# Moving the spectral pairs of batches 3 to 7 to fixed slots of a group

## The chip, the cores and the metric

The kernel runs on one core of one Trainium2 chip. The metric is the device time of one execution in microseconds (us); lower is better. Engines are named as in the profile: PE is TensorE (PEld its weight loads), DVE is VectorE, ACT is ScalarE, POOL is GpSimd and SP is SyncE. SP, ACT and POOL also issue the DMAs, each in the order of its own queue.

## The reference

Two blocks follow each other on x of 8 batches, 3136 positions and 256 channels. The first filters x along the sequence in the frequency domain; the second adds a low-rank product along the sequence and a two-layer network over the channels.

```python
def _attn_ref(x, filt_r, filt_i):
    X = np.fft.rfft(x, axis=1)
    F = (filt_r + 1j * filt_i)[None, :, :]
    return np.fft.irfft(X * F, n=x.shape[1], axis=1).astype(np.float32)

def _moe_ref(x, U, V, w_ch1, w_ch2):        # x is the first block's result
    xt = x.transpose(0, 2, 1)
    h = xt @ U @ V                          # U: 3136 x 32, V: 32 x 3136
    u = x + h.transpose(0, 2, 1)
    ch = np.maximum(u @ w_ch1, 0.0) @ w_ch2 # 256 -> 1024 -> 256
    return (u + ch).astype(np.float32)
```

## The kernel before

The Fourier transform of length 3136 = 64 x 49 is done as matrix products in float16, in stages. All of it is one instruction stream for each engine, whose order the kernel writes out by hand; nothing reorders it later.

**The stages of a batch.** `load_x` brings x in three chunks (POOL issues the DMAs). `f1_units` makes the first transform: one matmul into `pf` (L449) and one ACT copy (L455) per unit, 13 units, and after each chunk a store to the buffer `c1` in HBM (L459, from POOL). `load_a` (L468, from SP) reads `c1` back in another order, four blocks for each batch, all of which need the whole of `c1`. The middle stage takes 16 **pairs** of frequencies, four for each block. `stream` makes them one after another, and each pair consists of these steps:
- `forward`: two matmuls into `px` (L487), in a PSUM bank with the tag "x", of which there is one;
- `product`: three DVE multiplications with the filter read `px` (L506 once, L508 twice), and POOL adds the two halves to `y` (L511). Batch 1 uses `both_products` instead (one DVE instruction, L495);
- `i1`, two pairs later (`LAG = 2`): two matmuls with `y` into `pi` (L523), in the bank with the tag "f", of which there is one too, and an ACT copy to `esb` (L527). After four pairs SP stores `esb` to `c2` (L529).

`load_e` (L475, L480, from SP) reads `c2` back into the tiles `e2`. `h1_unit` then makes the batch's **low-rank sum** in three steps: 49 matmuls into `ph` (L563, also in the bank "f") and an ACT copy; a matmul and an ACT copy into `hz`; a DVE copy (L574) and four DMAs from SP (L580, L582, L585), which put the sum into rows 64 to 95 of `e2`.

**The groups.** The two-layer network goes over groups of 512 positions (8 rows of 64), six for each batch, and after each odd batch an **odd group** of the last row of two batches (128 columns). `make_u` builds u of a group (16 matmuls, L606, and two ACT copies). `mm1` makes one of eight blocks of hidden values: two matmuls into `phh` (L680) and a relu, on ACT (L688) or DVE (L686). The banks with the tag "m", of which there are four, hold `phh`, `pu`, `pf` and the second step's result. `mm2` makes the output of the group before in four steps. From batch 2 on it is `mm2_turned`, four matmuls in each step (L735); after its second and its fourth step DVE adds u (`tt`, L739) and transposes (L740), and after the fourth SP and POOL store the result. For batches 0 and 1 and for odd groups, `mm2` uses L706 and L710 and a DVE copy (L715); for an odd group only its first step does anything. The store of an odd group is two DMAs, one for each of its batches (L723).

**The order.** The main loop at the end of the kernel runs four steps for each group: `mm1` twice, `run(slot)`, in the third step `make_u` of the next group, a step of `mm2` of the group before, `run(slot + 1)`. So a full group has 8 slots, of which the even ones stand behind the two `mm1` and the odd ones behind the `mm2` step, and a batch has `SB = 48`. An odd group has no slots. What runs in a slot is put there in advance with `put`, and a slot runs its entries in the order in which they were put. The list `steps` holds the slot of each pair, from batch 1 on; the times of `load_a`, of `f1_units`, of `load_x` and of `load_e` are worked out from it, so that they move with it:

```python
for gi in range(NS // KG):
    t = steps[NP * (b - 1) + GP * gi]
    put(max(0, t - (14 if b > 3 else 9 + b // 3)), one(load_a, b, gi))
```

Before, the pairs of batch b stand in slots 48 (b - 2) + 18 + 3k, so that they take every slot of a group in turn. The low-rank sum's three steps stand 9, 8 and 7 slots ahead of the batch's first group.

Of the kernel before, what the change touches and what calls it, by code (L numbers as in the profile page):

```python
# [13 lines left out]
SEQ = 3136  # L14
NQ, NR = 64, 49
NS = 32
DM = 256
# [6 lines left out]
TB = 2  # L24
# [66 lines left out]
def kernel(  # L91
# [11 lines left out]
    nc = tc.nc  # L103
    nb = x.shape[0]
# [9 lines left out]
    RD = NR * DM  # L114
# [9 lines left out]
    def bank(tag, name):  # L124
        return ps.tile([128, 512], F32, tag=tag, bufs=BUFS[tag], name=name)
# [9 lines left out]
    def rows(ap, b, r, n):  # L135

        return bass.AP(tensor=ap.tensor, offset=ap.offset + (b * SEQ + r) * DM,
                       ap=[[RD, NQ], [1, n * DM]])

    def natural(ap):  # L140

        return ap.rearrange("p (r i h a) -> p r h i a", i=4, h=2, a=32)

    def split(ap):

        return ap.rearrange("p (r h i a) -> p r h i a", i=4, h=2, a=32)
# [104 lines left out]
    for h in range(2):  # L251
# [3 lines left out]
                    ap=[[64 * 1024, 4], [1024, 32], [1, 1024]]))  # L255
# [184 lines left out]
    def f1_units(b, both):  # L440
        ne = 0
        for c in range(len(CH)):
            xt = st[b]["x"].pop(c)
            asb = sb.tile([128, 9 * DM], F16, tag="asb", bufs=2, name="asb")
            for n0 in range(0, CH[c], 2):
                w = min(2, CH[c] - n0) * DM
                k = 64 if c0[c] + n0 == NH - 1 else 128
                pf = bank("o" if b == 1 else "m", "pf")
                nc.tensor.matmul(pf[:, 0:w], w64[:, :], xt[:, n0 * DM:n0 * DM + w],  # L449
                                 start=True, stop=True)  # L450
                dst = asb[0:k, n0 * DM:n0 * DM + w]
                if both and ne % 2 and (b > 1 or ne >= 9):
                    nc.vector.tensor_copy(dst, pf[0:k, 0:w])
                else:
                    nc.scalar.copy(dst, pf[0:k, 0:w])  # L455
                ne += 1
                if n0 + 2 >= CH[c]:
                    for h, o, n in span(c0[c], c0[c + 1]):
                        (nc.sync if b == 1 else nc.gpsimd).dma_start(c1[b].ap()[:, o:o + n], asb[64 * h:64 * h + 64, 0:n])  # L459
                yield  # L460
# [84 lines left out]
    def one(load, *a):  # L545
        load(*a)
        yield
# [78 lines left out]
    def turned(gx):  # L626

        return groups[gx][0] >= TB and groups[gx][2] > 1 and gx + 2 < len(groups)
# [46 lines left out]
    def mm1(gx, t):  # L675
        w = groups[gx][2] * 128
        ut = uts[gx]
        pm = bank("m", "phh")
        for dh in range(2):
            nc.tensor.matmul(pm[:, 0:w], w1[:, dh * 1024 + t * 128:dh * 1024 + (t + 1) * 128],  # L680
                             ut[:, dh * w:(dh + 1) * w], start=(dh == 0), stop=(dh == 1))
        h = sb.tile([128, 512], F16, tag="h", bufs=18, name="h")
        hs[gx, t] = h
        b = groups[gx][0]
        if t in ((4,) if b < TB or b == nb - 2 else () if b < nb - 1 else (1, 4, 6)):
            nc.vector.tensor_relu(h[:, 0:w], pm[:, 0:w])  # L686
        else:
            nc.scalar.activation(h[:, 0:w], pm[:, 0:w], RELU)  # L688

    def mm2(gx, rr):  # L690
        if gx < 0 or rr >= groups[gx][2]:
            return
        b, r0, nr = groups[gx]
        w = nr * 128
        if turned(gx):
            mm2_turned(gx, rr)
            return
        if rr == 0:
            ochs[gx] = (sb.tile([128, 4 * DM], F32, tag="och", bufs=2, name="och") if nr > 1 else
                        sb.tile([128, DM], F32, tag="ocho", bufs=1, name="ocho"))  # L700
        if rr % 2 == 0:
            pos[gx] = bank("o", "po")
        po, ut, och = pos[gx], uts[gx], ochs[gx]
        o = (rr % 2) * DM
        for t in range(8):
            nc.tensor.matmul(po[:, o:o + DM], hs[gx, t][:, rr * 128:(rr + 1) * 128],  # L706
                             w2[:, t * DM:(t + 1) * DM], start=(t == 0), stop=False,
                             skip_group_check=True)
        for dh in range(2):
            nc.tensor.matmul(po[:, o + dh * 128:o + (dh + 1) * 128],  # L710
                             ut[:, dh * w + rr * 128:dh * w + (rr + 1) * 128], idn[:, :],
                             start=False, stop=(dh == 1), skip_group_check=True)
        if rr % 2 or rr == nr - 1:
            a = (rr - rr % 2) * DM
            nc.vector.tensor_copy(natural(och[:, a:(rr + 1) * DM]), split(po[:, 0:(rr + 1) * DM - a]))  # L715
        if rr == nr - 1:
            for h in range(2):
                if nr == 1:
                    dst = rows(out, b - 1 + h, NR - 1, 1)
                else:  # L720
                    dst = rows(out, b, 2 * r0 + 4 * h, 4)
                eng = nc.gpsimd if b < nb - 1 else nc.scalar if gx + 2 >= len(groups) and h else nc.sync
                eng.dma_start(dst, och[64 * h:64 * h + 64, 0:nr * DM])  # L723

    def mm2_turned(gx, a):

        b, r0, _ = groups[gx]
        dh = a // 2
        if a == 0:
            ochs[gx] = sb.tile([128, 4 * DM], F32, tag="och", bufs=2, name="och")  # L730
        if a % 2 == 0:
            pos[gx] = bank("o", "po")
        po, och = pos[gx], ochs[gx]
        for t in range(4 * (a % 2), 4 * (a % 2) + 4):
            nc.tensor.matmul(po[:, :], w2[:, t * DM + dh * 128:t * DM + (dh + 1) * 128],  # L735
                             hs[gx, t][:, :], start=(t == 0), stop=(t == 7))
        if a % 2:
            tt = sb.tile([128, 512], F32, tag="tt", bufs=1, name="tt")
            nc.vector.tensor_add(tt, po[:, :], uts[gx][:, dh * 512:(dh + 1) * 512])  # L739
            nc.vector.transpose(och.rearrange("p (j h a) -> p h j a", h=2, a=32)[:, dh],  # L740
                                tt.rearrange("p (j t) -> p j t", t=32))
        if a == 3:
            for n in range(8):
                i, k = n // 2, n % 2
                dst = bass.AP(tensor=out.tensor,
                              offset=out.offset + (b * SEQ + 2 * r0) * DM + k * 32 * RD + i * 64,
                              ap=[[RD, 32], [DM, 8], [1, 64]])
                (nc.gpsimd if k and b < nb - 1 else nc.sync).dma_start(  # L748
                    dst, och[32 * i:32 * i + 32, k * 512:(k + 1) * 512]
                    .rearrange("p (r e) -> p r e", r=8))  # L750
# [3 lines left out]
    def put(slot, gen):  # L754
        sched.setdefault(int(slot + 0.5), []).append(gen)
# [6 lines left out]
    NP = NS // 2  # L762
    GP = NP // (NS // KG)
    SB = 48
# [17 lines left out]
    next(h1gen)  # L782
    make_u(0)

    steps = [7.6 + 1.3 * k for k in range(NP)] + [28 + 2.45 * k for k in range(NP)]
    for b in range(3, nb):
        steps += [SB * (b - 2) + 18 + 3 * k for k in range(NP)]
    steps += [steps[-1] + 3 * (k + 1) for k in range(LAG)]
    mid = stream()
    for k, t in enumerate(steps):  # L790
        put(t, mid)
        b, m = divmod(k - LAG, NP)
# [8 lines left out]
    for b in range(1, nb):  # L801
        for gi in range(NS // KG):
            t = steps[NP * (b - 1) + GP * gi]
            put(max(0, t - (14 if b > 3 else 9 + b // 3)), one(load_a, b, gi))
        gen = h1_unit(b)
        for t in (9, 8, 7):
            put(SB * b - t, gen)
        if b > 1:
            fill = f1_units(b, b == 2)
            t0 = steps[NP * (b - 1)]  # L810
            for k in range(NF):
                put(4 + 1.1 * k if b == 2 else 18 + 2.8 * k if b == 3 else t0 - 54 + 3 * k, fill)
            for c in range(len(CH)):
                if b > 2 or c > 0:
                    put(6 * c - 5 if b == 2 else 9 + 8 * c if b == 3 else t0 - 72 + 12 * c, one(load_x, b, c))
# [54 lines left out]
```

## Time and profile before

| | us |
|---|---|
| median of 3 runs | 544.36 |
| lowest and highest | 544.21, 546.55 |
| the profiled execution | 542.44 |
| its span, from the first to the last instruction | 540.7 |
| mean granted TensorE clock in it | 0.986 |

The profile shows one execution. Its busy times in stretches that end about where the low-rank sum of a batch stands (121 us for batch 1, 186 for batch 2, and so on, 475 for batch 7):

| stretch, us | length | PE busy | DVE busy | ACT busy | POOL busy | granted clock |
|---|---|---|---|---|---|---|
| 0 to 64 | 64 | 42.77 | 41.63 | 36.65 | 45.08 | 0.89 |
| 64 to 121 | 57 | 55.51 | 39.93 | 40.73 | 18.48 | 1.00 |
| 121 to 186 | 65 | 62.37 | 51.87 | 46.43 | 37.16 | 1.00 |
| 186 to 247 | 61 | 59.37 | 47.09 | 47.11 | 36.97 | 1.00 |
| 247 to 305 | 58 | 56.61 | 50.19 | 46.84 | 39.88 | 1.00 |
| 305 to 365 | 60 | 58.44 | 50.28 | 47.98 | 40.88 | 1.00 |
| 365 to 421 | 56 | 54.73 | 49.62 | 42.42 | 33.47 | 1.00 |
| 421 to 475 | 54 | 52.49 | 38.08 | 36.87 | 25.31 | 1.00 |
| 475 to 541 | 66 | 58.98 | 35.85 | 29.27 | 7.23 | 0.99 |

A line of a timeline gives the start, the time taken, the engine, the line of the kernel, the operation, what it writes and reads, sizes and count, and in brackets how long the engine was idle before it and who ended that. Matmuls are pipelined: a row's time reaches to its last result, while the next row starts earlier. A line of waits gives the engine and line, whom it waited for, the total in us, how often, and the longest.

### The profile page before, as it was taken

What the parts mean: (1) busy time and instruction counts of PE and PEld (TensorE: products, weight loads), DVE (VectorE), ACT (ScalarE), POOL (GpSimd) and SP (SyncE); (2) the same over time, 40 slices, a digit from 0 to 9 for tenths busy, and PEclk for the clock granted to TensorE, in tenths of its full rate; (3) what the DMA queues carried; (4) which work ended last, traced back from release to release, by engine and by line L of the source; (5) the groups of instructions that cost most, each with busy time, mean ns of one, the idle gap of its engine ahead of it and who ended that gap; (6) DMA issues with size and microseconds to landing.
All of it is one profiled execution on the core that took longest, in us unless ns stands there. A gap on an engine that the chain in (4) does not pass through costs nothing.

```text
span 540.7 us, 11254 instructions
## 1 busy us (share of the span) xinstructions
PE 501.3 (93%) x4022; PEld 305.0 (56%) x4022; DVE 404.5 (75%) x582; ACT 374.3 (69%) x762; POOL 284.5 (53%) x402
## 2 busy tenths in 40 slices
PE   4775999999999999999999999999999989999995
PEld 3664567767667675555555555555555555444444
DVE  6885267777887668887888788888899878445663
ACT  2766766677668668877788778887777577655541
POOL 7676532336645536675676666855656564313000
PEclk9978899999999999999999999999999999999999
DMA  8999998967889587987899797987776755644333
GB/s 132 203 188 198 177 218 223 239 191 165 210 237 232 146 182 196 187 222 185 185 229 229 178 203 203 229 204 156 183 185 150 161 118 130 139 90 79 78 70 97
DMA packets 118346, 94.98 MB, mean 176 GB/s; under 512 B 52817, under 2 KB 100626, under 8 KB 118290
## 3 DMA queue, kind: packets, MB, share of 16 engines
q0 software_dynamic: 21984, 42.52, 38.8%
q1 hardware_dynamic: 96146, 51.43, 37.4%
q8 instruction: 31, 0.51, 0.4%
q10 hardware_dynamic: 160, 0.33, 0.3%
q14 instruction: 25, 0.20, 0.1%
HBM read 57.25 MB, written 48.17 MB: 195 GB/s over the span
## 4 chain that ended last, share of the span: by engine, by line
PE 72%; DVE 9%; DMA 9%; ACT 5%; issue 3%; POOL 2%; SPq 0%; DVEq 0%; ACTq 0%; POOLq 0%
PE phh L680 25%; PE po L735 20%; PE po L706 7%; PE px L487 5%; DVE uv L508 4%; PE pi L523 4%; DMA xt<-in_x_dram 4%; PE pu L606 3%; PE pf L449 3%; PE ph L563 2%; DMA e<-e 2%; ACT h L688 2%; DVE uv L506 2%; DMA g<-gd 1%; DMA c<-asb 1%
## 5 line engine op out<-in xcount | busy, mean ns | idle before, releaser
L688 ACT ACTIVATE h<-phh 128x512 f16<-128x512 f32 (+1 forms) x376 | 198.5, 577 | 79.0 <-PE phh L680 74.2
L680 PE MATMUL phh<-ut,w 128*128 128x512 f16 x768 | 197.7, 379 | 1.8 <-ACT h L688 0.6
L511 POOL TENSOR_TENSOR y<-uv 128x512 f16<-128x512 f16 x96 | 111.2, 1160 | 110.8 <-DVE uv L508 65.1
L735 PE MATMUL po<-h,w 128*128 128x512 f16 x560 | 143.8, 379 | 0.0
L508 DVE TENSOR_TENSOR uv<-px,ft 64x512 f16<-64x512 f32 x192 | 132.2, 688 | 2.6
L680 PEld LDWEIGHTS <-w 128*128 128x128 f16 x832 | 78.3, 98 | 79.5 <-issue 4.6
L748 POOL DMA_DIRECT2D out_dram<-och x120 | 70.0, 591 | 47.3 <-DVE och L740 44.4
L527 ACT CAST esb<-pi 98x512 f16<-98x512 f32 x112 | 65.7, 587 | 37.9 <-PE pi L523 34.4
L506 DVE TENSOR_TENSOR uv<-px,ft 128x512 f16<-128x512 f32 x96 | 64.8, 675 | 26.6 <-PE px L487 23.9
L735 PEld LDWEIGHTS <-w 128*128 128x128 f16 x560 | 52.0, 98 | 52.8
L739 DVE TENSOR_TENSOR tt<-po,ut 128x512 f32<-128x512 f32 x70 | 48.4, 692 | 40.7 <-PE po L735 30.1
L706 PE MATMUL po<-w,h 128*128 128x256 f16 x448 | 58.1, 273 | 0.0
L487 PE MATMUL px<-a,t 98*128 98x256 f16 x256 | 49.8, 276 | 7.0 <-DVE uv L508 4.7
L455 ACT CAST asb<-pf 128x512 f16<-128x512 f32 (+1 forms) x83 | 48.0, 579 | 9.6 <-PE pf L449 7.6
L740 DVE STREAM_TRANSPOSE och<-tt 128x512 f32<-128x512 f32 x70 | 49.8, 712 | 2.4
L706 PEld LDWEIGHTS <-h 128*128 128x128 f16 x448 | 42.6, 98 | 10.2 <-issue 0.9
L495 DVE TENSOR_TENSOR uv<-px,ft 128x1024 f16<-128x1024 f32 x32 | 38.4, 1221 | 11.7 <-PE px L487 11.3
L487 PEld LDWEIGHTS <-t 98*128 98x128 f16 x256 | 22.0, 99 | 35.5 <-DVE uv L508 17.3
L449 PE MATMUL pf<-xt,w 128*128 128x512 f16 (+1 forms) x91 | 34.9, 385 | 5.5 <-DMA xt<-in_x_dram 4.4
L670 ACT CAST ut<-pu 128x512 f16<-128x512 f32 x70 | 38.1, 609 | 0.0
L523 PE MATMUL pi<-y,g 128*98 128x256 f16 x192 | 36.7, 272 | 0.6 <-POOL y L511 0.6
L155 POOL DMA_DIRECT2D xt<-in_x_dram x50 | 30.4, 613 | 5.3 <-DMA xt<-in_x_dram 2.1
(91 smaller groups left out, 449.0 us busy)
## 6 DMA issues: line engine op xcount, KB each, us to landing
xt<-in_x_dram POOLq DMA_DIRECT2D x46, 256.0 KB, 6.7
a<-c SPq DMA_DIRECT2D x28, 392.0 KB
c<-esb SPq DMA_DIRECT2D x28, 392.0 KB
e<-c SPq DMA_DIRECT2D x56, 192.0 KB
out_dram<-och SPq DMA_DIRECT2D x160, 64.0 KB
c<-asb POOLq DMA_DIRECT2D x30, 256.0 KB, 4.6
out_dram<-och POOLq DMA_DIRECT2D x120, 64.0 KB, 3.2
out_dram<-och POOLq DMA_DIRECT2D x24, 256.0 KB, 5.0
```

Of the source, the lines that this page charges most:

```text
L449: nc.tensor.matmul(pf[:, 0:w], w64[:, :], xt[:, n0 * DM:n0 * DM + w], start=True, stop=True)
L487: nc.tensor.matmul(px[:, sl * DM:(sl + 1) * DM], t2[:, s * 128:(s + 1) * 128], a2[:, (2 * ml + sl) * DM:(2 * ml + sl + 1) * DM], start=Tru ...
L506: nc.vector.tensor_mul(uv[:, 0:512], px[:, :], ft[:, a:a + 512])
L508: nc.vector.tensor_mul(uv[p:p + 64, 512:1024], px[q:q + 64, :], ft[q:q + 64, b:b + 512])
L511: nc.gpsimd.tensor_add(y, uv[:, 0:512], uv[:, 512:1024])
L523: nc.tensor.matmul(pi[0:98, sl * DM:(sl + 1) * DM], g12[:, g:g + 98], y[:, o:o + DM], start=(fi == 0), stop=(fi == nf - 1), skip_group_che ...
L527: nc.scalar.copy(split(esb[:, ml * 512:(ml + 1) * 512]), natural(pi[0:98, :]))
L680: nc.tensor.matmul(pm[:, 0:w], w1[:, dh * 1024 + t * 128:dh * 1024 + (t + 1) * 128], ut[:, dh * w:(dh + 1) * w], start=(dh == 0), stop=(dh ...
L688: nc.scalar.activation(h[:, 0:w], pm[:, 0:w], RELU)
L706: nc.tensor.matmul(po[:, o:o + DM], hs[gx, t][:, rr * 128:(rr + 1) * 128], w2[:, t * DM:(t + 1) * DM], start=(t == 0), stop=False, skip_gr ...
L735: nc.tensor.matmul(po[:, :], w2[:, t * DM + dh * 128:t * DM + (dh + 1) * 128], hs[gx, t][:, :], start=(t == 0), stop=(t == 7))
L748: (nc.gpsimd if k and b < nb - 1 else nc.sync).dma_start(dst, och[32 * i:32 * i + 32, k * 512:(k + 1) * 512] .rearrange("p (r e) -> p r e" ...
```

## The change

- The pairs of batches 3 to 7 stand at fixed slots. A cycle of three groups (24 slots) has eight pairs, at slots 0, 2 and 5 of the first group, 0, 2 and 5 of the second, and 0 and 4 of the third. A batch's first pair stands two slots earlier than before (48 (b - 2) + 16), its last one three slots earlier.
- The pairs of batch 2 start at slot 27 and are 2.4 slots apart, rounded, instead of 28 and 2.45.
- The low-rank sum of batches 2 to 7 stands 10, 9 and 8 slots ahead of the batch's first group, which makes its first step stand in slot 6 of a group instead of slot 7. That of batch 1 stays.
- All relus of batch 6 run on ACT. Before, one of eight ran on DVE.
- The store of an odd group is one DMA of 128 partitions instead of two of 64. It is issued from POOL, and the last one of the kernel from ACT, where before one half went from SP and one from ACT.

```diff
-        if t in ((4,) if b < TB or b == nb - 2 else () if b < nb - 1 else (1, 4, 6)):
+        if t in ((4,) if b < TB else () if b < nb - 1 else (1, 4, 6)):
             nc.vector.tensor_relu(h[:, 0:w], pm[:, 0:w])
...
-        if rr == nr - 1:
+        if rr == nr - 1 and nr == 1:
+            dst = bass.AP(tensor=out.tensor, offset=out.offset + ((b - 1) * SEQ + NR - 1) * DM,
+                          ap=[[SEQ * DM, 2], [RD, NQ], [1, DM]])
+            (nc.gpsimd if b < nb - 1 else nc.scalar).dma_start(dst, och[:, 0:DM])
+        elif rr == nr - 1:
             for h in range(2):
-                if nr == 1:
-                    dst = rows(out, b - 1 + h, NR - 1, 1)
-                else:
-                    dst = rows(out, b, 2 * r0 + 4 * h, 4)
+                dst = rows(out, b, 2 * r0 + 4 * h, 4)
                 eng = nc.gpsimd if b < nb - 1 else nc.scalar if gx + 2 >= len(groups) and h else nc.sync
...
-    steps = [7.6 + 1.3 * k for k in range(NP)] + [28 + 2.45 * k for k in range(NP)]
+    AT = (0, 2, 5, 8, 10, 13, 16, 20)
+    steps = [7.6 + 1.3 * k for k in range(NP)] + [27 + 2.4 * k for k in range(NP)]
     for b in range(3, nb):
-        steps += [SB * (b - 2) + 18 + 3 * k for k in range(NP)]
+        steps += [SB * (b - 2) + 16 + 24 * (k // 8) + AT[k % 8] for k in range(NP)]
...
-        for t in (9, 8, 7):
+        for t in (10, 9, 8) if b > 1 else (9, 8, 7):
             put(SB * b - t, gen)
```

## The prediction

> **What bounds the kernel now.** I read the page's busy shares first, then who TensorE waited for, then the timeline around those waits, then the last microseconds. The page:
>
> ```profile
> PE 501.3 (93%) x4022; PEld 305.0 (56%) x4022; DVE 404.5 (75%) x582; ACT 374.3 (69%) x762; POOL 284.5 (53%) x402
> ...
> PEclk9978899999999999999999999999999999999999
> ```
>
> TensorE (PE) is the long engine, and its clock is full from the sixth slice on. It issues in order, so a wait in front of one matmul goes straight into the time. The waits of PE's own rows:
>
> ```profile
> PE px L487 <- DVE uv L508: 4.7, 12, 1.2
> ...
> PE ph L563 <- ACT esb L527: 3.4, 5, 0.7
> ...
> PE pi L523 <- POOL y L511: 0.6, 1, 0.6
> ...
> PE phh L680 <- DVE h L686: 0.6, 1, 0.6
> ```
>
> These count only idle time of a PE that is drawn busy until its last result is out, so I measure a wait as the start of a block minus the start of the block before it and that block's issue time: four L680 or L735 matmuls take 0.86, a px or a pi 0.22, an f1 matmul (L449) 0.22, a make_u (16 x L606) 0.46, eight L706 with two L710 0.98. In the timeline of PE:
>
> ```profile
> 208.02 0.38 PE L487 MATMUL px<-a,t 98*128 98x256 f16 x2
> 208.24 0.38 PE L523 MATMUL pi<-y,g 128*98 128x256 f16 x2
> 208.46 1.02 PE L680 MATMUL phh<-ut,w 128*128 128x512 f16 x4
> 209.32 1.03 PE L735 MATMUL po<-h,w 128*128 128x512 f16 x4
> 210.66 0.39 PE L487 MATMUL px<-a,t 98*128 98x256 f16 x2 [0.31 <-DVE uv L508]
> ```
>
> The work between the two px is 0.43 + 0.86 + 0.86 = 2.15, their distance 2.64, so PE waited 0.48. The px bank is single and VectorE (DVE) must finish three products of it first: **two px are never closer than 2.64.** It takes longer when an output step stands before the products:
>
> ```profile
> 217.68 0.69 DVE L739 TENSOR_TENSOR tt<-po,ut 128x512 f32<-128x512 f32 x1 [0.97 <-ACT h L688]
> 218.41 0.71 DVE L740 STREAM_TRANSPOSE och<-tt 128x512 f32<-128x512 f32 x1
> 219.04 0.65 DVE L506 TENSOR_TENSOR uv<-px,ft 128x512 f16<-128x512 f32 x1
> 219.71 1.39 DVE L508 TENSOR_TENSOR uv<-px,ft 64x512 f16<-64x512 f32 x2
> ```
>
> Its px stood at 217.42 and the next came at 221.15, 3.73 later. Where the output step belongs to the group before, and px follows one pair of mm1 behind it (435.85 to 438.66, 320.62 to 323.43), the distance is 2.81.
>
> So read, the px waits of batch 2 are 0.9, of batches 3 to 7 2.1, 0.7, 1.4, 0.7, 2.1: **7.9 in all.** The low-rank sum:
>
> ```profile
> 303.54 0.38 PE L487 MATMUL px<-a,t 98*128 98x256 f16 x2
> 303.76 0.38 PE L523 MATMUL pi<-y,g 128*98 128x256 f16 x2
> ...
> 304.82 1.38 PE L563 MATMUL ph<-e,ul 64*32 64x256 f16 x44 [0.67 <-ACT esb L527]
> ```
>
> ph and pi share the one bank f, so ph waits for ScalarE's copy of the pi just issued: 0.83 each, in batches 2 to 6 (at 185, 246, 304, 364, 420): 4.2. At 440.9 and 442.0, in batch 6, PE waited 0.44 and 0.72 for relus: 1.2. At 236.1 it waited 0.77 for y. All else from 121 us on is small.
>
> **The change, part by part.** Its cost depends on the PE work between two px, which I counted in the order of the changed kernel's instructions.
>
> *Slots 0, 2, 5.* From slot 0 to slot 2 there are a px and pi, four L735 and four L680: 2.15, or 2.37 with an f1 matmul between. Both are under 2.64. At slot 0 the output step of the group before stands ahead of the products, as in the 2.81 rows; adding its steps from E, the end of the last L735 block (tt starts at E + 0.26, uv 1.36 later, px stands at E + 0.86), gives 2.86, so I take 2.83. Each such wait is 0.46 with an f1 matmul, 0.68 without. From 2 to 5 PE has 3.69 and from 5 to 8 3.23, in the third group 4.1 and 4.6: no wait there, since uv at slot 5 comes 0.1 after the transposes.
> - Batches 4 and 6 have four two-slot distances: 0.46 + 0.46 + 0.36 (behind ph and pn, which give DVE 0.1) + 0.68 = 1.96 each.
> - Batches 3, 5 and 7 run over an odd group. In the group behind it mm2 has only a step 0, so distances shrink: 2.28, then 1.76 (slot 2 to 5: four L680 and a make_u), then 2.15. Against 2.64 that is 0.37 + 0.88 + 0.49 = 1.74, with the 2.81 start 1.9.
> - Batch 5: 0.46 + 0.46 + 0.36 + 1.9 = 3.2. Batch 7, which has no f1 work beside it: 0.68 + 0.58 + 1.9, and 0.91 at the second group, where without an f1 matmul tt waits for the products of slot 5 and ends 0.2 later: 4.1. Batch 3 has the short output copies of batches 0 and 1 beside it: three distances of 2.49 give 0.45, the odd group 1.74. It also starts one slot after the last pair of batch 2, as before, but now just behind an output copy: 2.94 (the distance that 169.70, at such a slot, would need) - 1.29 = 1.65, where before has 1.34. Together 3.8.
> - Batch 2 (steps 27 + 2.4k): distances of 2.49 (four), 2.28 and 2.85: 1.1.
>
> Sum 16.1 against 7.9: **+8.2.** With 2.64 everywhere it would be 12.9, **+5.0**: the lower bound.
>
> *Batch 2 starting at 27.* Slot 27 now holds the last pair of batch 1 as well, with 0.65 of PE work between. Before, with 1.51 between, the second px came 2.08 after the first (102.46 to 104.54, 0.57 waited). Now 1.43: **+0.9** (+0.5 if DVE frees it at 1.7).
>
> *Low-rank sum in slot 6.* The pair before it stands in slot 4, a make_u and two blocks (2.2) earlier, so the copy of pi is long done: five waits fall away. Batch 1's sum stays at slot 39, and there a pair now falls into the same slot just ahead of it: one wait comes. **-3.3.** The copies (L574) and their DMAs on SP go one slot earlier with it. In the DVE queue L574 (0.7) now stands between the products of slots 0 and 2: those of slot 2 start 0.2 later and still end before slot 5 needs them. PE waited 0.4 for the copied rows once, in batch 1, which is unchanged.
>
> *Relus of batch 6.* Six of 0.63 leave DVE, six of 0.58 join ScalarE, which is busy 37 of 54 us there. The two waits go: **-1.2**, bound 0 if ScalarE is then the late one.
>
> *y.* POOL's two-pair lag is now at least 5 slots, not 6: slot 0 to slot 5 is 6.5 us, against 2.8 for the products, some 2.4 of store issue (4 x 0.59) running beside them, and 1.2 for y. I let the one wait go: **-0.8**, bound +0.5 if two x loads (0.6 each) get ahead as well.
>
> *One last store.*
>
> ```profile
> 534.21 0.56 ACTq L723 DMA_DIRECT2D out_dram<-och  x1
> 534.44 0.55 SPq L723 DMA_DIRECT2D out_dram<-och  x1
> ...
> 534.93 0.48 ACTq L723 DMA_DIRECT2D out_dram<-ocho  x1
> ...
> 537.38 0.49 SPq L723 DMA_DIRECT2D out_dram<-ocho  x1
> ```
>
> SP's half of the last rows was issued 2.45 after ScalarE's half, because it waits on the completion semaphore that ScalarE's och store still holds. With one store from ScalarE that issue is gone; what is late next is the landing of the same och store (about 537.3) and of the ocho store behind it on that queue, about 0.5 later, where SP's landed about 1 after 537.9. **-0.8**, bounds 0 and -2.4. The Trainium skill (DMA: Bandwidth & Descriptors, section Issuing engines are not separate DMA queues) says that issuing from several engines saves only the sequencer's time. By that alone the merge is worth one issue, 0.5, and the sum would be 0.3 higher; no run here shows yet which it is.
>
> **Sum:** 8.2 + 0.9 - 3.3 - 1.2 - 0.8 - 0.8 = +3.0. The profiled execution took 542.44 (span 540.7 and 1.7 around it), so it would take 545.4. The median of the runs is 544.36, 1.9 above it; that spread I leave as it is: **547.4.** Bounds together: +5.0 + 0.5 - 3.3 - 1.2 - 0.8 - 2.4 = -2.2 and 8.2 + 0.9 - 3.3 + 0 + 0.5 + 0 = +6.3.
>
> **The rivals.**
> 1. *Only the bare 2.64 counts*: the output step never delays the products. 3.0 - 3.2 = -0.2: 544.2. For it: many px rows show uv at px + 0.49. Against: the 2.81 rows have just the geometry of slot 0. Chance 0.25.
> 2. *The other side: ScalarE paces the short distances.* If PE reaches the second px late anyhow, since its relus hold the four m banks, the new px waits cost nothing: px stays at 7.9, the sum is -5.2 and the time 539.2. It decides where four blocks take over 2.64 instead of 2.15. For: ScalarE ran without a gap from 204.9 to 211.3 behind the odd group. Against: PE waited only 0.6 in all for ScalarE's relus, ScalarE 74.2 for PE. Chance 0.10.
> 3. *A load is late.* Pairs of batch 3 come two slots (2.4) earlier, but their first block cannot leave before c1 has landed, and that write has not moved. Before, it was issued at 146.99 and used at 158.88. If it takes all of that, batch 3 waits 2.4 more: 549.8. No PE row waits for such a load now. Chance 0.13.
> 4. *The clock falls.* In the first 64 us, with waits of 3, the clock granted was 0.89; from 64 on, with waits up to 1.34, it was 1.00. If bunched waits bring 0.89 back in three odd stretches of 8 us, 3 us more: 550.4. The Trainium skill (TensorE: Matmul & The Clock Gate, A second HAM failure mode: psum-queue depth-cycling) has a kernel where short idles between matmul groups made the clock swing; this trace does not bear it out, with some 25 such idles at 1.00. Chance 0.04.
>
> **How the numbers follow.** My forecast has 0.48, with its own range 545.5 to 549. A measurement of this kernel tells about 0.5% (2.7 us) from no change, so slower begins at 547.1, inside it: 0.30 of it is slower, 0.18 same. Rival 1 is same (0.23, the rest slower), 2 faster, 3 and 4 slower: slower 0.30 + 0.02 + 0.13 + 0.04 = 0.49, same 0.41, faster 0.10. From 543.0 to 551.0 leaves out rival 2 and the far end of 3 and 4.
>
> **What would show it.** Right: px at slot 2 some 2.8 behind px at slot 0 in every 0, 2, 5 group; px distances of 2.64 three in a row behind odd groups; no ph wait except the one of batch 1; SP's last issue an och store. Wrong: px waits from 121 us on below 12; waits of PE on ScalarE's relus above 2; any px that waits for a DMA; a granted clock below 1.00 after 64 us.

## The result

| | before | changed |
|---|---|---|
| median of 22 runs each, us | 543.51 | 547.05 |
| lowest and highest, us | 541.63, 549.32 | 544.76, 550.17 |
| the profiled execution, us | 542.44 | 547.96 |
| its span, us | 540.7 | 546.2 |
| mean granted clock in it | 0.986 | 0.981 |

The changed kernel takes 1.0064 times as long, with an interval of 1.0042 to 1.0087: slower by 3.5 us, somewhere between 2.3 and 4.7. The two profiled executions differ by more, 5.5, since that of before lies 1.1 under its median and the other 0.9 above its own. The lower mean clock comes from the first 64 us, 0.84 against 0.89, where both kernels have the same instructions; from there on the granted clock is 1.00 in the changed kernel.

The page of the changed kernel, the busy shares and the clock by slices. Lines of the kernel from the stores on are numbered one higher than before (L735 is L736, L739 L740, L740 L741, L748 L749; the odd group's store was L723 and is L719, and L724 is the other store of that kind):

```profile
PE 502.3 (92%) x4022; PEld 304.0 (56%) x4022; DVE 400.4 (73%) x576; ACT 378.6 (69%) x768; POOL 284.9 (52%) x399
...
PEclk9688899999999999999999999999999999999999
```

The work of PE is the same, 4022 matmuls, and 1.0 us more of it drawn busy. DVE has six instructions less and ACT six more, which are batch 6's relus; POOL has three less, the stores of three odd groups. So most of the 5.5 us must be waits of PE. In the waits of PE's own rows (us in all, how often, the longest):

```profile
PE px L487 <- DVE uv L508: 11.3, 25, 1.3
...
PE px L487 <- DVE uv L495: 1.7, 2, 1.3
...
PE pu L606 <- DVE h L686: 1.1, 1, 1.1
...
PE ph L563 <- ACT esb L527: 0.7, 1, 0.7
```

`px` stood at 4.7 behind L508 and 12 times; now it is 11.3 and 25 times. `ph` is down from five waits to one, and the two rows for `y` and for batch 6's relus on DVE are gone. Another row has come, a `make_u` that waits for a relu on DVE. A usual stretch with the pairs of slots 0 and 2, PE and then DVE:

```profile
223.04 0.38 PE L487 MATMUL px<-a,t 98*128 98x256 f16 x2
223.26 0.38 PE L523 MATMUL pi<-y,g 128*98 128x256 f16 x2
223.48 0.38 PE L449 MATMUL pf<-xt,w 128*128 128x512 f16 x1
223.69 1.03 PE L736 MATMUL po<-h,w 128*128 128x512 f16 x4
224.56 1.03 PE L680 MATMUL phh<-ut,w 128*128 128x512 f16 x4
225.91 0.39 PE L487 MATMUL px<-a,t 98*128 98x256 f16 x2 [0.32 <-DVE uv L508]
```

```profile
222.43 0.69 DVE L740 TENSOR_TENSOR tt<-po,ut 128x512 f32<-128x512 f32 x1 [1.15 <-ACT h L688]
223.16 0.71 DVE L741 STREAM_TRANSPOSE och<-tt 128x512 f32<-128x512 f32 x1
223.79 0.65 DVE L506 TENSOR_TENSOR uv<-px,ft 128x512 f16<-128x512 f32 x1
224.46 1.39 DVE L508 TENSOR_TENSOR uv<-px,ft 64x512 f16<-64x512 f32 x2
```

Slot 0 puts `px` at 223.04, but DVE is still at the output step of the group before; its three products run from 223.79 to 225.85, and the `px` of slot 2 starts at 225.91. The distance is 2.87, the work between 2.38: 0.49 waited. Behind an odd group the bank alone sets the distance, three times in a row, as in these two:

```profile
211.69 0.39 PE L487 MATMUL px<-a,t 98*128 98x256 f16 x2 [0.71 <-DVE uv L508]
...
214.34 0.39 PE L487 MATMUL px<-a,t 98*128 98x256 f16 x2 [0.31 <-DVE uv L508]
```

Those are 2.65 apart, and the first of them 2.65 behind the one at 209.04; PE waited 0.36, 0.87 and 0.47. The low-rank sum of batch 4, at 304.82 with a wait in front of it before, is an example of the five that went. That of batch 3, which waited 0.83 as well (at 247.36), now reads:

```profile
249.79 0.40 PE L563 MATMUL ph<-e,ul 64*32 64x256 f16 x8
```

No bracket: no pair stands just ahead of it now. The end of the kernel, DMA issues on ScalarE's and SyncE's queues:

```profile
539.99 0.58 ACTq L724 DMA_DIRECT2D out_dram<-och  x1
540.05 0.55 SPq L724 DMA_DIRECT2D out_dram<-och  x1
...
540.71 0.50 ACTq L719 DMA_DIRECT2D out_dram<-ocho  x1
```

The late half on SP is gone, and SP's last issue is an `och` store. The last packets of the one `ocho` store landed at 544.32, 3.1 after its issue was done; before, SP's half landed 1.1 after its issue. From PE's last result to the end it is 5.98, and was 6.24.

### The profile page after: what moved, and what is told of

Its sections match the earlier page's. It is cut to its first block, busy times and chain, and to the rows that moved or that the text cites. A ratio compares the mean times of both kernels' runs of the same rounds, so it can differ in the third digit from the quotient of the medians.

```text
span 546.2 us, 11249 instructions
## 1 busy us (share of the span) xinstructions
PE 502.3 (92%) x4022; PEld 304.0 (56%) x4022; DVE 400.4 (73%) x576; ACT 378.6 (69%) x768; POOL 284.9 (52%) x399
## 5 line engine op out<-in xcount | busy, mean ns | idle before, releaser
L736 PE MATMUL po<-h,w 128*128 128x512 f16 x560 | 143.8, 379 | 0.0
L508 DVE TENSOR_TENSOR uv<-px,ft 64x512 f16<-64x512 f32 x192 | 132.1, 688 | 2.5
L749 POOL DMA_DIRECT2D out_dram<-och x120 | 70.7, 596 | 56.3 <-DVE och L741 53.6
L740 DVE TENSOR_TENSOR tt<-po,ut 128x512 f32<-128x512 f32 x70 | 48.4, 692 | 57.8 <-PE po L736 35.0
L736 PEld LDWEIGHTS <-w 128*128 128x128 f16 x560 | 51.5, 97 | 48.4 <-issue 1.1
L487 PE MATMUL px<-a,t 98*128 98x256 f16 x256 | 50.3, 279 | 15.9 <-DVE uv L508 11.3
L741 DVE STREAM_TRANSPOSE och<-tt 128x512 f32<-128x512 f32 x70 | 49.8, 712 | 2.4
L495 DVE TENSOR_TENSOR uv<-px,ft 128x1024 f16<-128x1024 f32 x32 | 38.4, 1221 | 11.3 <-PE px L487 11.0
```

What stands on the lines that cost most here:

```text
L487: nc.tensor.matmul(px[:, sl * DM:(sl + 1) * DM], t2[:, s * 128:(s + 1) * 128], a2[:, (2 * ml + sl) * DM:(2 * ml + sl + 1) * DM], start=Tru ...
L508: nc.vector.tensor_mul(uv[p:p + 64, 512:1024], px[q:q + 64, :], ft[q:q + 64, b:b + 512])
L749: (nc.gpsimd if k and b < nb - 1 else nc.sync).dma_start(dst, och[32 * i:32 * i + 32, k * 512:(k + 1) * 512] .rearrange("p (r e) -> p r e" ...
```

## The experiments

Times are ratios to the kernel before, run beside each on the same chip, with intervals; 0.1% is 0.54 us. "px waits" are those from 121 us on, by start-to-start distances as in the prediction: 7.87 in before, 16.42 in the changed kernel.

**e1: the changed kernel with the old steps.**

```diff
-    steps = [7.6 + 1.3 * k for k in range(NP)] + [27 + 2.4 * k for k in range(NP)]
+    steps = [7.6 + 1.3 * k for k in range(NP)] + [28 + 2.45 * k for k in range(NP)]
-        steps += [SB * (b - 2) + 16 + 24 * (k // 8) + AT[k % 8] for k in range(NP)]
+        steps += [SB * (b - 2) + 18 + 3 * k for k in range(NP)]
```

> The changed kernel with the pairs at their old steps (28 + 2.45 k; then every third slot from 18 on); low-rank sum in slot 6, batch 6's relus on ScalarE and the one store stay. My theory (the slots cost 8 to 9 us of px waits, the rest of the change gains): px waits from 121 us on back at 7.9, no ph wait (no pair stands in slot 39, so batch 1 has none either: -4.2), no relu wait in batch 6 (-1.2), the tail 0.3 shorter: about 5.5 us faster than before, ratio 0.990. Rival (the rest of the change, relus on ScalarE or the earlier low-rank sum, costs too): no faster than before.

Measured: 0.9947 (0.991 to 0.9985). So the other parts together are a gain, and the steps turn it into a loss: 1.0064 less 0.9947 is 1.17%, 6.4 us. The gain is smaller than expected. All `ph` waits and the relu waits are gone, but px waits are 9.42, not 7.9. Four new ones of 0.37 to 0.59 stand at the pair right behind the low-rank sum, as in the timeline of PE in this kernel:

```profile
248.09 0.38 PE L487 MATMUL px<-a,t 98*128 98x256 f16 x2
...
251.82 0.38 PE L487 MATMUL px<-a,t 98*128 98x256 f16 x2 [0.21 <-DVE uv L508]
```

These are 3.73 apart, which is what DVE needs with an output step ahead of the products. Before, PE spent part of that in front of `ph`; without that wait it reaches the next `px` earlier and waits there.

**e2: the steps alone, in the kernel before.** (`AT` and the two lines for `steps`, nothing else.)

> The kernel before with only the pairs moved (27 + 2.4 k; 0, 2, 5, 0, 2, 5, 0, 4). Theory: px waits 16.4 instead of 7.9 (+8.5), the shared slot 27 +0.9, a relu on VectorE that holds up make_u in batch 1 about +1; and since no pair stands in slot 7 or just ahead of it either, the ph waits of batches 2 to 6 go by the pairs alone, with batch 1's new one: -3.3; y -0.8; the relu waits of batch 6 stay. Sum about +6: 1.011. Rival (the ph waits need the low-rank sum to be moved): five ph waits of 0.83 stay in the trace, sum about +9.5.

Measured: 1.0131 (1.0076 to 1.0186), as expected. px waits 15.5. The five `ph` waits on ScalarE are gone here too, though the low-rank sum stays in slot 7: the new steps have no pair there. In the changed kernel, then, moving the sum removes no `ph` wait of its own. The `make_u` wait for a relu on DVE (1.1) is in this kernel as well. Its profiled execution has in addition a `ph` of batch 1 that waits 3.0 in pieces for the read of `c2`; that of e6 has 2.1 of the kind, e9 0.6, the changed kernel none, and I ascribe it to no edit.

**e3: the changed kernel with a second px bank, taken from the four of "m".**

```diff
-    BUFS = {"x": 1, "f": 1, "m": 4, "o": 2}
+    BUFS = {"x": 2, "f": 1, "m": 3, "o": 2}
```

> The changed kernel with two PSUM banks for px and three instead of four for the hidden values (tag m). Theory (the waits come from the single px bank): px waits of 16.4 fall below 3, PE then may wait for relus or for the copies of ScalarE, since three banks hold less; if that costs under 5, the kernel comes out 9 to 13 us faster than the changed one. Rival 1 (VectorE itself is too slow for pairs so close, the bank only shows it): the waits move to pi behind y or to the banks of po, and the time stays near the changed kernel's. Rival 2: the m banks were the tight resource; slower.

Measured: 1.0106 (1.0052 to 1.016), no gain. The px waits are 0.00, and PE waits elsewhere, by its rows:

```profile
PE pu L606 <- ACT h L688: 5.8, 15, 0.6
PE pu L606 <- DVE h L686: 2.4, 2, 1.3
```

By start distances, waits for relus (`make_u` and `mm1`) from 121 us on are 17.8, against 2.4 in the changed kernel: 16.4 went and 15.4 came. Of these, 4.05 stand in the last batch, which has no pairs and had nearly no waits. So my main expectation, a gain, failed: the bank that was taken from "m" is missed there. Rival 1 falls too, since VectorE keeps up with pairs so close. From slot 0 to slot 2, where the changed kernel takes 2.87, it is now the bare 2.38 of PE work:

```profile
222.34 0.38 PE L487 MATMUL px<-a,t 98*128 98x256 f16 x2
...
224.73 0.38 PE L487 MATMUL px<-a,t 98*128 98x256 f16 x2
```

VectorE's three products are the same here, and no `pi` waits for `y`. No run has three "m" banks and one `px` bank, so how much of the 15.4 those three banks cost by themselves stays open beyond the 4.05.

**e4: the changed kernel with even distances of three slots, from the new early start.**

```diff
-        steps += [SB * (b - 2) + 16 + 24 * (k // 8) + AT[k % 8] for k in range(NP)]
+        steps += [SB * (b - 2) + 16 + 3 * k for k in range(NP)]
```

> The changed kernel with the early start (first pair of a batch at 16, batch 2 as changed) but pairs at every third slot, not at 0, 2, 5. Theory (distances of two slots cost): px waits about 9 (odd groups 1.4 each, batch 2 and its end 2.5, the rest single waits behind output steps), 7 us under the changed kernel. Rival (it is the early start, by loads and DMA traffic, not the distances): stays within 2 us of the changed kernel, and px rows wait for a DMA.

Measured: 0.9993 (0.996 to 1.0026), px waits 11.75. Against the changed kernel that is 0.71% less, 3.9 us, and 4.7 less of px waits. So of the 6.4 us between e1 and the changed kernel, some 3.9 are the uneven distances, and 2.5 the early start and batch 2's steps. Each is uncertain by 2 to 3 us, so the second alone is not clear of nothing; the px waits divide in the same way, 4.7 and 2.3. The direction was expected, the size was 7.

**e5 and e6: the second product as one DVE instruction over 128 partitions, in the changed kernel and in the one before.**

```diff
-        for p, q in ((0, 64), (64, 0)):
-            nc.vector.tensor_mul(uv[p:p + 64, 512:1024], px[q:q + 64, :],
-                                 ft[q:q + 64, b:b + 512])
+        nc.vector.tensor_mul(uv[:, 512:1024], px[:, :], ft[:, b:b + 512])
```

> The changed kernel with the second product of batches 2 to 7 made by one VectorE instruction over 128 partitions instead of two over 64 (it leaves out the exchange of the two halves, so the result is not the reference's). Each px is then held 0.7 us less: 1.95 instead of 2.64, 2.15 instead of 2.85 behind an output step, both under the 2.15 to 2.37 of the two-slot distances. Theory (the waits come from the time that VectorE holds the one px bank): px waits from 121 us on fall from 16.4 to 2 or 3, the time by 13 to 14 us against the changed kernel, to a ratio of about 0.981 to the kernel before, and under the same edit of the kernel before (next run). Rival (the close pairs cost by something else, such as ScalarE's or POOL's turn or the loads): the distance of 3.5 us to the same edit of the kernel before stays.

> The kernel before with the same edit of the second product (it too leaves out the exchange of halves). Theory: px waits from 7.9 to about 1, ph waits (4.2) and the relu waits stay; ratio about 0.987. The changed kernel with this edit should be 3 to 4 us faster than this one, where without the edit it is 3.5 us slower.

Measured: e5 0.9742 (0.969 to 0.9793), e6 0.9847 (0.9794 to 0.99). The groups show why the bank comes free sooner: a product over 64 partitions takes 688 ns and there are two, one over 128 takes 678. px waits are about 1.0 and 0.5. Against the changed kernel e5 is 17.5 us faster (14 to 21), where 13 to 14 were expected and 15.4 of px waits went. The stretch behind the odd group, at the same place as above, now has next to no wait (PE, kernel e5):

```profile
208.21 0.38 PE L487 MATMUL px<-a,t 98*128 98x256 f16 x2
...
210.04 0.39 PE L487 MATMUL px<-a,t 98*128 98x256 f16 x2
```

That is 1.84 apart instead of 2.65; a wait of under 0.1 is left. And the sign turns: 0.9742 over 0.9847 is 0.989 (0.982 to 0.997, taking the two intervals as independent), where the two kernels without this edit stand at 1.0064. So the change as a whole is the better version when DVE holds `px` for two products, and the worse one with three. The comparison is of the whole change, not of the slots alone: what the low-rank sum, the relus and the store gain is in it. The edit also takes work from DVE, and not only time from the bank; that it is the bank which counts is what e3 adds, where DVE's work stayed and the px waits went.

**e7: only the last pair of a cycle off the even grid, from the old start.**

```diff
-    AT = (0, 2, 5, 8, 10, 13, 16, 20)
-    steps = [7.6 + 1.3 * k for k in range(NP)] + [27 + 2.4 * k for k in range(NP)]
+    AT = (0, 3, 6, 9, 12, 15, 18, 20)
+    steps = [7.6 + 1.3 * k for k in range(NP)] + [28 + 2.4 * k for k in range(NP)]
-        steps += [SB * (b - 2) + 16 + 24 * (k // 8) + AT[k % 8] for k in range(NP)]
+        steps += [SB * (b - 2) + 18 + 24 * (k // 8) + AT[k % 8] for k in range(NP)]
-        for t in (10, 9, 8) if b > 1 else (9, 8, 7):
+        for t in (9, 8, 7):
```

> A version meant to beat both: store and relus as in the changed kernel, low-rank sum at its old 9, 8, 7 slots, pairs at every third slot from 18 on, except that the eighth of a cycle stands one slot earlier (20 instead of 21), so that none stands in slot 7 of a third group, where the output step delays its products by 1.1, nor with ph; batch 2 at 28 + 2.4 k, so that it ends two slots ahead of batch 3, not one. Theory: the px waits of 0.4 to 0.5 behind such pairs (two in a batch) and 1.2 of the 1.34 at batch 3's start go, px waits from 121 us on 3 to 5; ph waits 0 to 0.3 (pi stands 1.08 ahead of ph, 1.05 are needed); 5 to 7 us faster than before, ratio 0.988. Rival (VectorE is the bound, and a wait that is removed in one place comes back at the next pair): px waits stay at 8 to 9 and the ratio at that of the old steps, 0.995.

Measured: 0.9933 (0.9899 to 0.9968): faster than both kernels, and not to be told from e1. px waits on DVE are 8.2, not the 3 to 5 that I hoped for: the wait for DVE at the start of batch 3 is gone (in the profiled execution, the slowest of its twelve, that pair waits 1.1 for its load), and other pairs wait instead. DVE has little slack there. Eight pairs (2.12 each, from start to start) and six output steps (1.36) of a 24-slot cycle are 25.1 us of DVE work, and the PE work of the same cycle is about 27.3 (25.6 without f1 matmuls).

**e8 and e9: the kernel before with only the low-rank sum moved, and with only batch 6's relus on ScalarE and one store for each odd group.** The edits are those lines of the change.

> The kernel before with only the low-rank sum moved to slot 6. Theory: the five ph waits (4.2) go; about 0.37 comes back at the next pair in each of four batches (with the old steps it stands in slot 7 behind ph, and the output step then delays its products), as it did when the relus and the store were changed too; net 2.5 to 3 us faster, ratio 0.995. Rival (the ph waits were cover for other work and all of it comes back): px waits from 7.9 to 11 or more, ratio 1.000.

> The kernel before with only batch 6's relus on ScalarE and one store for each odd group. Theory: the two waits of 1.16 in batch 6 go, the time from TensorE's last result to the end falls by 0.3: 1.5 us faster, ratio 0.997, which five rounds may not tell from 1. Rival (ScalarE becomes late in batch 6): new waits of TensorE for ScalarE's relus there, no gain.

Measured: e8 0.9969 (0.9938 to 1.0001), which is not quite clear of no change, and e9 0.996 (0.9928 to 0.9991). In e8 4.2 of `ph` waits go and px waits grow to 9.61, so 1.7 of 4.2 is given back, as in e1. In e9 the relu waits go, px waits stay (7.71), no wait for ScalarE comes, and the time behind PE's last result is 5.91. The parts, +1.31% (e2), -0.31% and -0.40%, add up to +0.6%, and the changed kernel measured +0.64%; but that proves little. e2 and e8 lose the same `ph` waits, so that the sum counts them twice; without e8 it is +0.9%, and e2's interval of 0.55% either way holds both.

## Why the prediction was right

It said 547.4 and slower, and slower it was, mainly for the reason it gave; one term was mis-sized and one missing. That 547.4 lies 0.35 from the measured 547.05 is in part luck. Its base, the median of three runs, was 0.85 above the median of 22, and its sum, +3.0, was 0.5 under the measured difference: the two cancel in part. The terms as the two profiled executions show them also come to more than +3.0, as the count below shows.

- **The px waits**, its largest term, +8.2: measured 16.42 less 7.87, **+8.55**. By batch, 2 to 7: 1.1, 3.8, 1.96, 3.2, 1.96 and 4.1 were worked out, and 0.9, 3.6, 2.15, 3.2, 2.5 and 4.05 measured. The distances it rested on were 2.83 from slot 0 to slot 2 (mostly 2.87 measured, 2.76 to 3.20 in batches 4 to 7), 2.64 behind odd groups (2.65), and 1.65 waited at the start of batch 3 (1.50). Most of what batch 6 has too much is one distance of 3.20, at 355.21: there the output step waits for the products of slot 5, which the prediction had counted for batch 7 alone. e3, e5 and e6 show that the hold of the one bank by three products is the cause: with a second bank or a shorter hold the term is gone, and with the shorter hold the sign turns.
- **Slot 27**, +0.9: PE waited 1.42 at 105.65, where the same pair waited 0.55 before, **+0.87**.
- **The low-rank sum**, -3.3: five waits of 0.83 went and the one of batch 1 came, **-3.35**. The size was right, the owner was not: e2 loses those waits by its steps alone. With the old steps, where moving the sum does count, e8 shows 1.7 of it lost to DVE, which the prediction had not looked for.
- **Relus of batch 6**, -1.2, and **y**, -0.8: both waits are gone.
- **One last store**, -0.8: **mis-sized, -0.26**. The stall of 2.45 on SP is gone, as the step said, but the landing that comes next was put at 0.5 behind the `och` store. One store of 128 KB, queued behind 512 KB of `och` (all issued within 1.2 us), lands 3.1 after its issue. In the four kernels with two stores (before, e2, e6, e8) it is 6.24 to 6.26 from PE's last result to the end, and in the seven with one store 5.86 to 5.99: some 0.3. The Trainium skill (DMA: Bandwidth & Descriptors, Issuing engines are not separate DMA queues) says that DMAs of all issuers run on the same engines and interleave there. The trace agrees: ScalarE's and SyncE's `och` stores were issued 0.06 apart, and their packets run from 541.23 to 543.02 and from 542.59 to 543.97, those of the `ocho` store from 543.13 to 544.32. The prediction's other estimate by that section, -0.5, is nearer.
- **Not in the sum: a `make_u` that waits 1.22.** DVE and then PE:

```profile
172.67 0.69 DVE L506 TENSOR_TENSOR uv<-px,ft 128x512 f16<-128x512 f32 x1 [0.56 <-PE px L487]
173.37 1.39 DVE L508 TENSOR_TENSOR uv<-px,ft 64x512 f16<-64x512 f32 x2
174.79 0.69 DVE L715 COPY och<-po 128x512 f32<-128x512 f32 x1
175.40 0.68 DVE L686 TENSOR_SCALAR h<-phh 128x512 f16<-128x512 f32 x1
```

```profile
176.13 0.39 PE L606 MATMUL pu<-low,e 96*128 96x64 f16 x8 [1.05 <-DVE h L686]
```

In batch 1 one relu of eight is still on DVE. Two pairs two slots apart now stand ahead of it, it runs late, and the "m" bank that it empties is the one `make_u` needs. e2 has this wait too, e4 with its even distances has not. The prediction followed only `px` through the DVE queue, and not what else stands in it.

The terms as measured, 8.55 + 0.87 - 3.35 - 1.2 - 0.8 - 0.26 + 1.22, make +5.0. A `make_u` at 481.78 that waited 0.62 for a relu waits 0.18 in the changed kernel and in e9: 0.4 less, which gives +4.6. That is 1.6 above the prediction's sum and at the upper end of the 2.3 to 4.7 between the medians. The spans differ by 5.5 since the execution of the changed kernel was 1.1 late already at 70.5, 0.8 of it at a `px` that waited for the load of its block. Those 1.1 I don't ascribe to the change: up to there the instructions are the same, and that wait comes and goes between profiled executions (0.84 in e1, none in e8 and e9).

**The rivals.** That only the bare 2.64 counts gave 544.2, and falls with the distances of 2.87. That ScalarE paces the short distances gave 539.2, and falls: PE's waits for ScalarE's relus came to 1.2 at most from 121 us on. They do grow when "m" has three banks (e3), so the idea was sound, but with four it does not come to that. That a load is late: no `px` of batch 2 or later waits for a load in the changed kernel; the one at 70.5 is of batch 1, which the change does not move. In e7's profiled execution two of batches 3 and 5 do, 1.1 and 2.1, so that margin is small. That the clock falls: it is 1.00 from 64 us on, with 27 waits of `px` behind DVE. The swing of the clock with short idles between matmul groups that the Trainium skill reports of another kernel (TensorE: Matmul & The Clock Gate, A second HAM failure mode: psum-queue depth-cycling) does not show here, with idles of up to 1.3 us between matmul groups.

## What to carry to other kernels

Before moving instructions of an in-order engine closer together, find how long their buffer is held, by whom, and what can stand ahead of the holder in its queue; then work out the distance of every neighbouring pair, not the mean. A wait that is removed can come back at the next thing that depends on a busy engine, here 1.7 of 4.2 us; and a bank that is taken from another stage can cost there what it gains, here 15.4 of 16.4. So follow the whole queue of the busy engine, and prefer to shorten the holder's work. Parts of one change can have opposite signs: here e1 without the new steps, and e7 with a milder form of them, are 0.5 to 0.7% faster than before, while all together are 0.6% slower.

## What the runs showed of the hardware

- A DVE multiply from PSUM costs the same over 64 partitions as over 128 (688 and 678 ns for 512 elements each). Splitting a product by partitions doubles its time, and the time its bank is held: `px` distances fall from 2.65 to 1.84 without the split.
- Merging two 64-partition stores into one of 128 saved only some 0.3 us at the end, although one of the two had been issued 2.45 us late. Its packets started only at 543.13, when the 512 KB ahead of it were nearly through (543.97).
- Some 30 idles of up to 1.3 us in front of matmuls, from 64 us on, left the granted clock at 1.00.
